# Attention and a gated convolution on one core: tiles 5 to 7 take the product with v on quarters of the array, with a new order of all work

## The chip, the cores and the metric

The kernel runs on one core of one Trainium2 chip. The metric is the device time of one execution in microseconds (us). Three runs of the kernel before gave 554.05, 554.26 and 555.79 us; the median is 554.26 us.

## The reference

Inputs are q, k and v (8 batches, 8 heads, 576 positions, 64 numbers a head) and three weights. What is computed, in short:

```python
scores = scale * q @ k.T                      # per batch and head
scores = where((rel >= 0) & (rel < 128), scores + slope[h] * -abs(rel), -1e9)
attn = exp(scores - max) ; attn = attn / (sum(attn) + 1e-9)
x = (attn @ v)                                # heads side by side: 576 x 512 per batch
h = maximum(x @ w_in, 0)                      # 512 -> 1024
conv = sum over 3 taps of conv_w[k] * h shifted by k - 1
out = (h * sigmoid(conv)) @ w_out             # 1024 -> 512
```

A position sees itself and the 127 positions before it, so a tile of 128 positions needs the keys of its own tile and of the tile before.

## The kernel before, in words

The 8 x 576 positions are 36 tiles of 128. For each tile the kernel turns q and k so that the head dimension lies on partitions, takes the scores (`scores`, L398 and L413), adds the position's bias (`add_bias`, L473, VectorE), takes exps (L481, ScalarE), normalises, turns the weights so that keys lie on partitions, and takes the product with v (`av`). The result is x, written as a high and a low part into `ring` (`x_hi`, `x_lo`). The network then runs on blocks of 256 positions, each in four steps of 256 of the 1024 features: up-projection (`up`, L692 and L697, name UH; its last number is the half of the step's features), relu (HH), convolution (Z, CA, CB, L732), tanh (TH), gate (GT), its high and low part (GH, GL), down-projection (`down`, L794 for the first steps, L804 later, name D), and after four steps the store of the output (OB, L830). The down-projection is TensorE's largest work.

Tiles before `FIRST` = 8 turn their weights on TensorE (`attnT`, L507) into the tiles `rl`; from tile 8 on the weights are turned by VectorE and through DRAM (TE, WE, SE, CE, tiles `eb`, `scr`, `rr`, `ll`). q and k are turned on TensorE before tile 8 (QU, L351, copied out by QV) and from tile 8 on by VectorE's transposes (`turn`, name TQ, L365) from the tiles `rp_late`, which small loads fill four at a time (LG, L315). The loads of q and k for the tiles before 8 are LD and LH, those of v LV (L341), of the weights F (L197).

The product with v exists in two forms. The old one (L631, tiles before 8) takes for each head and each of the two key tiles one product of 128 keys by 64 columns of v, all into one PSUM bank. `av_quarters` (L591, tiles from 8) cuts the array into four quarters of 64 by 64: the two key halves and two heads run beside each other, each key half into a PSUM bank of its own, and parts that the mask makes zero are left out. The two banks are then summed: ScalarE copies the first to the tile `xx` (XA, `x_part`, L186) and VectorE adds the second (XS, `x_sum`, L605). In the old form `x_hi` copies from PSUM and `x_lo` subtracts on VectorE (L659); in the quarter form `x_hi` copies from `xx` and `x_lo` subtracts on GpSimd (L657).

The order is written by hand: three lists of pieces, which `emit` walks, so that each engine and each DMA queue runs its instructions in the order of the list. OPENING has the first tiles, the preparation of weights and eleven steps' up-projections; PERIOD is emitted 14 times for two tiles and four steps each; TAIL ends the work. A name in the set `OTHER` puts that piece on its other engine (`pick`). `MB3.0.0` is piece MB on tile 3, with two indices of its own; in PERIOD the first number is added to the period's own tile or step. I is a spin, four matmuls on the identity that keep TensorE at work. SP issues all DMAs in the list's order.

Of the kernel before, what the change touches and what calls it, by code (L numbers as in the profile page):

```python
# [22 lines left out]
def tile_alibi_window_attention_conv_glu(  # L23
# [357 lines left out]
    def scores(t, u):  # L381
        if t >= TURN:
            if u == 0:
                for half in range(2):
                    scores_window(t, half)
            return
# [491 lines left out]
    LH0.0 LH0.1 LD1 F0 QU0.0 QU0.1 QV0.0 S0.0 MP0.0.0 F4 MP0.0.1 MB0.0.0 QV0.1 S0.1 LD2 MP0.1.1 LD3 MB0.0.1 MP0.1.0  # L878
    MB0.1.1 QU1.0 QU1.1 I2 QV1.0 I2 I2 LW0 MB0.1.0 S1.0 MP1.0.1 CL4 MP1.0.0 QV1.1 S1.1 MP1.1.0 MB1.1.0 MB1.0.1 QU2.1
    X0.0.0 X0.0.1 X0.1.1 X0.1.0 NR0 QV2.1 X1.1.0 N0.0 I1 I1 N0.1 X1.0.1 LW4 QU2.0 QV2.0 S2.1 MB1.0.0 CL0 S2.0  # L880
    MP1.1.1 X1.0.0 MB1.1.1 T0.1 RS4 X1.1.1 F1 CL1 LW1 MP2.1.1 MP2.0.0 MP2.0.1 NR1 T0.0 RL0.0 RL0.1 N1.1 N1.0 F2
    SEL0.0 V4 QU3.1 MB2.1.1 I1 I1 LV2 MB2.0.0 QV3.1 MP2.1.0 MB2.1.0 MB2.0.1 RS0 QU3.0 QV3.0 T1.1 P4 S3.1 SEL0.1
    MP3.1.0 MP3.1.1 RL1.1 MB3.1.0 SEL1.1 V0 S3.0 T1.0 RL1.0 LD4 QU4.0 X2.0.1 MB3.1.1 W4 I2 X2.1.1 CL2 MP3.0.1 X2.1.0
    QU4.1 LV0 X2.0.0 NR2 N2.1 N2.0 F3 AV0 XH0 QV4.1 QV4.0 MB3.0.1 H0 T2.0 RL2.0 LW3 X3.1.1 S4.0 MP3.0.0 MB3.0.0 T2.1
    LD5 S4.1 SEL1.0 CL3 SEL2.0 MP4.0.1 MB4.0.1 RL2.1 RS1 V1 RS3 RS2 LW2 MP4.0.0 SEL2.1 QU5.1 LV1 AV1 QV5.1 AV2 F6
    CL6 S5.1 XH1 QU5.0 MP4.1.0 MB4.1.0 X3.0.0 V3 X3.0.1 F8 MP4.1.1 MB4.1.1 MB4.0.0 CL8 X3.1.0 V2 F5 CL5 XH2 XL2 H1
    QV5.0 RS8 W1 LG4 UH1.0 NR3 N3.0 N3.1 MP5.1.1 UH1.1 X4.0.1 MP5.1.0 T3.1 HH1.0 X4.1.0 MB5.1.1 UH0.0 F7 CL7 LW5 W0
    MB5.1.0 F15 HH0.0 LW8 X4.1.1 X4.0.0 NR4 RL3.1 RS6 LD6 QU6.1 LW6 V6 LW7 RS7 V7 T3.0 QV6.1 V8 N4.0 LG4 LV4 RS5 V5
    HH1.1 RL3.0 SEL3.0 UH0.1 S5.0 MP5.0.0 HH0.1 LV3 F10 CL10 Z0.1 QU6.0 MP5.0.1 H7 F9 Z0.0 T4.0 RL4.0 H3 CA0.1 CB0.1
    LG4 UH3.0 HH3.0 N4.1 UH2.0 SEL4.0 CA0.0 T4.1 CB0.0 MB5.0.1 LD7 CL9 SEL3.1 X5.1.1 QV6.0 S6.0 MB5.0.0 HH2.0 TH0  # L890
    RL4.1 RS10 SEL4.1 X5.1.0 GT0 MP6.0.0 S6.1 MB6.0.0 Z1.0 MP6.0.1 AV3 H2 W3 X5.0.0 LW10 LG4 MP6.1.1 Z1.1 MB6.0.1
    LW9 AV4 H8 QU7.1 CA1.0 CB1.0 F12 LG4 X5.0.1 MP6.1.0 MB6.1.0 CA1.1 W2 CB1.1 NR5 N5.1 LV5 UH3.1 XH4 XL4 RS9 V9
# [5 lines left out]
    CA4.0 CB4.0 T6.0 TQ8 LG4 X7.0.1 RL5.0 LG4 UH6.0 TH4 GT4 LG4 LG4 GL2 LG4 SEL5.0 RL6.0 SEL6.0 V16 H16 T6.1 RL6.1
    SEL6.1 LW14 LG4 LG4 Z5.1 CA5.1 LG4 LG4 CB5.1 RS14 HH6 Z5.0 CA5.0 D1 CB5.0 RS15 RS13 AV5 XH5 HH7 GH4 BW0 V13 XL5
    V14 N7.0 AV6 XH6 TH5 GT5 Z6.0 S8.0 D2 LV9 H9 Z6.1 MP8.1.1 MB8.1.1 MP8.1.0 H12 V15 H15 LG4 LG4 CA6.1 MB8.1.0 T7.0  # L900
    RL7.0 D3 CB6.1 XL6 UH8.1 UH8.0 LG4 TQ9 X8.1.0 CA6.0 CB6.0 H14 UH9.1 W16 MP8.0.0 MB8.0.0 H11 W11 TH6 GT6 W9 H13
    GL4 Z7.1 CA7.1 CB7.1 MP8.0.1 Z7.0 HH8 MB8.0.1 W14 CA7.0 GH5 CB7.0 W13 X8.1.1 GL5 N8.1 TE8.1 S9.0 MP9.1.0 MP9.0.1
# [59 lines left out]
```

## Time and profile before

| what | value |
|---|---|
| median of three runs | 554.26 us |
| the profiled execution | 554.5 us |
| its span on the core | 552.8 us |
| TensorE busy | 546.0 us, 99% |
| VectorE, ScalarE, GpSimd busy | 446.8, 384.4, 342.5 us |
| mean granted TensorE clock | 0.999 |

The profiled execution's own time is 1.7 us above its span: what lies around the span. TensorE's matmuls are pipelined, so a busy TensorE need not be one at its peak. Engines other than TensorE matter where TensorE waits for them.

### The profile page before, as it was taken

The page shows a single profiled execution, that of the slowest core. Times are in us where ns is not written, and L with a number is a line of the kernel's source. Part 1 is how long each engine was busy: PE and PEld are TensorE (multiplying, and loading weights), DVE is VectorE, ACT ScalarE, POOL GpSimd, SP SyncE. Part 2 cuts the span into 40 slices and gives each one's busy share as a digit, 9 for nine tenths or more (in the row PEclk, how much of TensorE's full clock was granted, in tenths as well). Part 3 has the DMA queues.
Part 4 walks back from the last instruction along what each step waited for, and adds up shares of the span by engine and source line. Part 5 has one row for each costly group of instructions (what it writes and reads, how often), then busy time and mean ns, then how long its engine had stood idle before and what let it go on. Part 6 is the DMA issues. An engine that isn't in the chain of part 4 may idle for free.

```text
span 552.8 us, 17956 instructions
## 1 busy us (share of the span) xinstructions
PE 546.0 (99%) x6689; PEld 479.2 (87%) x6689; DVE 446.8 (81%) x1505; ACT 384.4 (70%) x1149; POOL 342.5 (62%) x450
## 2 busy tenths in 40 slices
PE   9999999999999999999999999999999999999997
PEld 8788886988888888888888888898989898989986
DVE  8899999888789977887596987788879987665763
ACT  5899876775867676868586776767676777664441
POOL 1787977594656575666558493948473948483241
PEclk9999999999999999999999999999999999999999
DMA  9987764546776767767676768676768664540102
GB/s 209 229 242 204 202 104 81 164 156 169 157 205 142 231 156 205 184 205 169 183 201 175 196 178 207 163 219 184 190 176 205 179 162 148 159 155 1 39 0 78
DMA packets 206779, 91.39 MB, mean 165 GB/s; under 512 B 178380, under 2 KB 192996, under 8 KB 206692
## 3 DMA queue, kind: packets, MB, share of 16 engines
q1 hardware_dynamic: 206692, 90.24, 62.5%
q8 instruction: 53, 0.87, 0.7%
q14 instruction: 34, 0.28, 0.2%
HBM read 51.40 MB, written 38.80 MB: 163 GB/s over the span
## 4 chain that ended last, share of the span: by engine, by line
PE 91%; DMA 2%; DVE 2%; SPq 2%; issue 1%; ACT 0%; DVEq 0%
PE o L804 34%; PE p L697 33%; PE av L591 7%; PE sc L413 6%; PE p L692 3%; PE o L794 3%; PE av L631 3%; PE sc L398 2%; SPq L341 1%; DMA wst<-in_moe_w_in_dram 1%; PE pa L507 1%; PE pt L351 1%; DVE zp L732 1%; DMA rp_late<-in_q_dram 1%; SPq L315 0%
## 5 line engine op out<-in xcount | busy, mean ns | idle before, releaser
L697 PE MATMUL p<-ring,wi 128*128 128x256 f32 x1088 | 195.8, 282 | 0.7 <-ACT hh L709 0.7
L732 DVE SCALAR_TENSOR_TENSOR zp<-hh,cw,zp 128x256 f32<-128x256 f32 (+7 forms) x384 | 160.4, 418 | 29.2 <-ACT zp L717 19.6
L697 PEld LDWEIGHTS p<-ring,wi 128*128 128x128 f32 x1088 | 168.4, 188 | 4.9 <-ACT hh L709 1.1
L697 PE MATMUL p<-ring,wl 128*128 128x256 f32 x544 | 152.3, 280 | 0.0
L768 POOL TENSOR_TENSOR gl<-z,gh 128x512 fp32r<-128x512 f32 x63 | 81.5, 1294 | 100.9 <-ACT gh L186 68.4
L481 ACT ACTIVATE e<-e,st 128x128 f32<-128x128 f32 x288 | 111.8, 391 | 4.2 <-DVE st L473 3.1
L804 PE MATMUL o<-wo,gh 128*128 128x512 f32 x270 | 110.0, 407 | 0.0
L501 POOL TENSOR_TENSOR e<-e,st 128x512 f32<-128x512 f32 x69 | 72.2, 1056 | 58.9 <-DVE st L493 54.1
L804 PE MATMUL o<-wo,gl 128*128 128x512 f32 x270 | 105.7, 392 | 0.0
L804 PE MATMUL o<-wl,gh 128*128 128x512 f32 x270 | 105.2, 390 | 0.0
L697 PEld LDWEIGHTS p<-ring,wl 128*128 128x128 f32 x544 | 102.7, 189 | 0.0
L739 ACT ACTIVATE zp<-zp 128x512 f32<-128x512 f32 (+1 forms) x73 | 42.2, 578 | 62.9 <-DVE zp L732 61.5
L717 ACT ACTIVATE zp<-hh,cw 128x256 f32<-128x256 f32 x144 | 68.5, 476 | 20.0 <-DVE z L747 10.0
L473 DVE CUSTOM_DVE_ANT_0 e<-sc,bias 128x128 f32<-128x128 f32 x288 | 66.8, 284 | 1.7 <-PE pa L507 0.2
L747 DVE SCALAR_TENSOR_TENSOR z<-zp,hh 128x512 f32<-128x512 f32 (+1 forms) x73 | 49.0, 671 | 21.1 <-ACT zp L739 20.2
L804 PEld LDWEIGHTS o<-wo,gh 128*128 128x128 f32 x270 | 50.6, 188 | 16.6 <-issue 6.7
L804 PEld LDWEIGHTS o<-wo,gl 128*128 128x128 f32 x270 | 50.5, 187 | 11.5
L804 PEld LDWEIGHTS o<-wl,gh 128*128 128x128 f32 x270 | 50.8, 188 | 9.3
L709 ACT ACTIVATE hh<-p 128x512 f32<-128x512 f32 (+2 forms) x69 | 39.5, 572 | 25.2 <-PE p L697 20.3
L481 ACT ACTIVATION_READ_ACCUMULATOR e<-e,st 128x1 f32 x288 | 54.5, 189 | 0.0
L186 ACT CAST gh<-z 128x512 fp32r<-128x512 f32 x58 | 35.6, 614 | 15.3 <-DVE z L747 15.3
L572 POOL TENSOR_SCALAR_AFFINE_SELECT rr<-rr 128x512 f32<-128x512 f32 x56 | 40.2, 722 | 3.4
(131 smaller groups left out, 882.5 us busy)
## 6 DMA issues: line engine op xcount, KB each, us to landing
scr<-eb SPq DMA_DIRECT2D x28, 1024.0 KB, 5.1
rr<-scr SPq DMA_DIRECT2D x112, 128.0 KB, 3.7
out_dram<-ob SPq DMA_DIRECT2D x17, 512.0 KB, 3.4
rv<-in_v_dram SPq DMA_DIRECT2D x32, 256.0 KB, 3.4
rp_late<-in_k_dram SPq DMA_DIRECT2D x192, 36.0 KB, 2.9
rp_late<-in_q_dram SPq DMA_DIRECT2D x192, 36.0 KB, 2.2
wst<-in_moe_w_in_dram SPq DMA_DIRECT2D x8, 512.0 KB, 7.0
wst<-in_moe_w_out_dram SPq DMA_DIRECT2D x8, 512.0 KB, 4.8
```

Of the source, the lines that this page charges most:

```text
L473: nc.vector.tensor_tensor_reduce(out=e[:, j, :], in0=of[:, g, :], in1=bias[:, u * HU + j, :], scale=-0.125, scalar=FAR, op0=ALU.add, op1=A ...
L481: nc.scalar.activation(out=e[:, j, :], in_=e[:, j, :], func=AF.Exp, bias=st[:, 0, j : j + 1], scale=-1.0, accum_out=st[:, 1, j : j + 1],)
L501: eng.tensor_tensor(out=e, in0=e, in1=st[:, 2, :].unsqueeze(2).to_broadcast([P, HU, P]), op=ALU.mult)
L572: nc.gpsimd.affine_select(out=r, in_=r, pattern=[[BK, 2], [0, H], [1, BK]], compare_op=ALU.is_ge, fill=0.0, base=q0, channel_multiplier=-1,)
L697: nc.tensor.matmul(ps, a[:, part], ring[:, i, cc, cols], start=cc == 0 and n == 0, stop=cc == NCC - 1 and n == 2)
L709: nc.scalar.activation(out=to, in_=ps, func=AF.Relu, scale=0.5)
L717: nc.scalar.activation(out=zps[s][:, ff, :], in_=hhs[s][:, ff, 1 : 1 + CW], func=AF.Copy, scale=cw[:, 1, f : f + 1])
L732: nc.vector.scalar_tensor_tensor(out=z[:, ff, a:cut], in0=hh[:, ff, a + kk : cut + kk], scalar=cw[:, kk, f : f + 1], in1=z[:, ff, a:cut], ...
L739: nc.scalar.activation(out=zps[s][:, ff], in_=zps[s][:, ff], func=AF.Tanh)
L747: nc.vector.scalar_tensor_tensor(out=zgs[s][:, ff], in0=zps[s][:, ff], scalar=1.0, in1=hhs[s][:, ff, 1 : 1 + CW], op0=ALU.add, op1=ALU.mult,)
L768: eng.tensor_tensor(out=gl, in0=zgs.pop(s), in1=as32(gh), op=ALU.subtract)
L804: nc.tensor.matmul(to, a[:, ff, ms], w[:, part], start=first and n == 0, stop=end and n == 2)
```

## The change

The product with v of tiles 5, 6 and 7 takes the quarter form. Their weights are still turned on TensorE, so the quarters read from `rl` through a new function `part_of`. The limits of `av`, `x_part`, `x_sum`, `x_hi` and `x_lo` go from `FIRST` (8) to `QUARTERS` (5). `TURN` and `SOLO` are 8, as `FIRST` is, and only give names to conditions that stay as they were. OPENING gets the pieces XA5, XS5, XA6 and XS6 (tile 7's are in the first period already), and all three lists and `OTHER` are ordered anew.

```diff
-    TURN = FIRST
+    TURN = 8
+    SOLO = 8
+    QUARTERS = 5
...
+    def part_of(t, side, h, rows, c, n):
+        if t >= FIRST:
+            return sides_of[t][side][rows, c // BK : (c + n) // BK, h, :]
+        return rls[t, h // HU][rows, side, h % HU, c : c + n]
...
                             vraw[t - side][rows, h + a],
-                            sides_of[t][side][rows, c // BK : (c + n) // BK, h + a, :],
+                            part_of(t, side, h + a, rows, c, n),
...
     def x_sum(t):
-        if t < FIRST:
+        if t < QUARTERS:
             return
...
     def x_part(t):
-        if t >= FIRST:
+        if t >= QUARTERS:
...
     def av(t):
-        if t >= FIRST:
+        if t >= QUARTERS:
             av_quarters(t)
             return
...
     def x_hi(t):
         ps, hi, lo = avs[t]
-        if t >= FIRST:
+        if t >= QUARTERS:
             copy_on(pick(nc.scalar, nc.gpsimd), hi, xs[t])
             return
...
         ps, hi, lo = avs.pop(t)
-        if t >= FIRST:
+        if t >= QUARTERS:
             pick(nc.gpsimd, nc.vector).tensor_tensor(out=lo, in0=xs.pop(t), in1=as32(hi), op=ALU.subtract)
             return
...
     OTHER = set(
...
-        QV2.0 QV3.0 RL1.0 RL3.1 RL5.1 RL6.1 T:GH-1 T:GH0 T:GH1 T:GH2 T:GH3 T:GH4 T:GH5.0 T:GH5.1 T:GL-1 T:GL0
...
+        GH7 GH8 GL5 H10 H11 H13 H3 H5 H6 H9 HH1.0 KC9 LW0 LW1 LW11 LW12 LW14 LW4 LW6 LW7 N4.1 N5.0 N8.0 N8.1
+        N9.0 P:GH0 QV3.0 QV4.0 QV7.0 RL0.1 RL6.0 T:GH-1 T:GH0 T:GH1 T:GH5.1 T:GL-1 T:GL1 T:GL3 T:GL5.0 T:GL5.1
+        T:HH0 T:HH5.0 T:OB1 T:OB5 T:XA-1 T:XH-1 W0 W13 XH0 XH2 XH5
...
     OPENING = """
...
+    SEL6.1 V16 HH6 LG4 Z5.1 LG4 SEL6.0 LG4 AV6 RS14 CA5.1 LG4 H16 LG4 LG4 H11 LG4 RS13 S8.0 V13 XA5 BW0 XS5 V15 XH5
+    XL5 LG4 XA6 XS6 XH6 X7.0.1 V14 D2 CB5.1 TH5 GT5 XL6 MP8.0.0 N7.0 Z6.0 H9 MP8.0.1 LG4 LG4 UH8.0 H14 MP8.1.1 CA6.0
...
     PERIOD = """
-    OB0 HH0 Z0.0 MB2.0.1 MB2.0.0 X2.0.0 UH1.1 UH1.0 HH1 X2.0.1 CA0.0 AV-1 TQ3 CB0.0 XA-1 XS-1 AV0 LG4 GH-1 GL-1 N2.0
...
+    HH0 UH1.0 MB2.0.0 Z0.0 UH1.1 MB2.0.1 HH1 GH-1 GL-1 X2.0.0 CA0.0 CB0.0 TQ3 Z0.1 LG4 AV-1 XA-1 XS-1 X2.0.1 CA0.1
...
     TAIL = """
...
+    UH1.0 HH0 Z0.0 CA0.0 AV-1 D-2 XA-1 XS-1 XH-1 Z0.1 CA0.1 XL-1 CB0.1 UH1.1 XF-1 UH3.0 CB0.0 TH0 UH2.1 HH1 GH-1 GT0
```

The order moves instructions at three places that matter below. The first is SP's queue in the opening, from its fifth DMA on (`rp_` tiles hold q and k, `wst_` a weight's words, `rv_` v). Before:

```order
L341 DMA rp_169<-in_q_dram 128x8x64
L341 DMA rp_169<-in_k_dram 128x8x64
L197 DMA wst_176<-in_moe_w_in_dram 128x1024
L197 DMA wst_199<-in_moe_conv_w_dram 24x256
L341 DMA rp_211<-in_q_dram 128x8x64
L341 DMA rp_211<-in_k_dram 128x8x64
L341 DMA rp_211<-in_q_dram 128x8x64
L341 DMA rp_211<-in_k_dram 128x8x64
L197 DMA wst_343<-in_moe_w_in_dram 128x1024
L197 DMA wst_366<-in_moe_w_in_dram 128x1024
L341 DMA rv_380<-in_v_dram 128x8x64
```

After the change:

```order
L197 DMA wst_187<-in_moe_conv_w_dram 24x256
L343 DMA rp_169<-in_q_dram 128x8x64
L343 DMA rp_169<-in_k_dram 128x8x64
L343 DMA rp_227<-in_q_dram 128x8x64
L343 DMA rp_227<-in_k_dram 128x8x64
L197 DMA wst_241<-in_moe_w_in_dram 128x1024
L197 DMA wst_273<-in_moe_w_in_dram 128x1024
L343 DMA rp_227<-in_q_dram 128x8x64
L343 DMA rp_227<-in_k_dram 128x8x64
L343 DMA rp_301<-in_q_dram 64x8x64 x2
L343 DMA rp_301<-in_k_dram 64x8x64 x2
L197 DMA wst_306<-in_moe_w_in_dram 128x1024
L343 DMA rv_358<-in_v_dram 128x8x64
```

The first full block of w_in (`wst_176`) leaves its place ahead of tile 1's q and k, and the next two blocks now stand ahead of tile 3's loads instead of behind them.

The second place is VectorE in the opening around the products of tiles 5 and 6 (`av_1367` and `av_1399` before, `av_1_1306` and `av_1_1371` now; L659 and L611 are lines of x's low part and of the sum; L225 prepares weights). Before:

```order
L188 COPY rl_1_1328<-pa_1_1323 128x512
L221 TENSOR_SCALAR wst_1010<-wst_1010 128x512
L732 SCALAR_TENSOR_TENSOR zp_1341<-hh_164,cw,zp_1341 128x256 x4
L225 SCALAR_TENSOR_TENSOR wg_1365<-wg_1365,wst_1002 128x512
L659 TENSOR_TENSOR ring<-av_1367,ring 128x4x128
L225 SCALAR_TENSOR_TENSOR wg_1353<-wg_1353,wst_1010 128x512
L493 RECIPROCAL st_0_1122<-st_0_1122 128x4
L188 CAST ring<-av_1399 128x4x128
L747 SCALAR_TENSOR_TENSOR z_1418<-zp_1341,hh_164 128x512
```

After the change:

```order
L221 TENSOR_SCALAR wst_1101<-wst_1101 128x512
L738 SCALAR_TENSOR_TENSOR zp_1286<-hh_164,cw,zp_1286 128x256
L225 SCALAR_TENSOR_TENSOR wg_1349<-wg_1349,wst_1147 128x512
L738 SCALAR_TENSOR_TENSOR zp_1286<-hh_164,cw,zp_1286 128x256
L225 SCALAR_TENSOR_TENSOR wg_1426<-wg_1426,wst_1038 128x512
L611 TENSOR_TENSOR xx<-xx,av_1_1306 128x512
L225 SCALAR_TENSOR_TENSOR wg_1299<-wg_1299,wst_722 128x512
L611 TENSOR_TENSOR xx<-xx,av_1_1371 128x512
L225 SCALAR_TENSOR_TENSOR wg_1404<-wg_1404,wst_1101 128x512
L738 SCALAR_TENSOR_TENSOR zp_1286<-hh_164,cw,zp_1286 128x256
L753 SCALAR_TENSOR_TENSOR z_1491<-zp_1286,hh_164 128x512
```

The two subtractions of L659 have left VectorE (the second stands a few rows below the piece shown), and two additions from PSUM (L611) stand in their place, among the same preparation of weights.

The third place is SP's queue in a period: loads of q (`rp_late`), of v, the store of an output block of 512 KB (`out_dram`), and the trip of the turned weights through DRAM (`scr`, `rr`). Before:

```order
L315 DMA rp_late<-in_q_dram 32x9x32 x4
L341 DMA rv_2294<-in_v_dram 128x8x64
L315 DMA rp_late<-in_q_dram 32x9x32 x12
L830 DMA out_dram<-ob_2352 128x2x512
L544 DMA scr_2375<-eb_2356 256x1x1024
L315 DMA rp_late<-in_k_dram 32x9x32 x8
```

After the change:

```order
L317 DMA rp_late<-in_q_dram 32x9x32 x4
L343 DMA rv_2411<-in_v_dram 128x8x64
L317 DMA rp_late<-in_q_dram 32x9x32 x8
L836 DMA out_dram<-ob_2424 128x2x512
L317 DMA rp_late<-in_q_dram 32x9x32 x4
L545 DMA scr_2442<-eb_2404 256x1x1024
L317 DMA rp_late<-in_k_dram 32x9x32 x8
```

Four of the period's q loads have moved from ahead of the output store to behind it. Everything else of the queue has kept its order.

## Rows read from the trace of the kernel before

**Rows 1.** The page, busy time by engine, clock by slices, chain by engine.

```profile
PE 546.0 (99%) x6689; PEld 479.2 (87%) x6689; DVE 446.8 (81%) x1505; ACT 384.4 (70%) x1149; POOL 342.5 (62%) x450
...
PEclk9999999999999999999999999999999999999999
...
PE 91%; DMA 2%; DVE 2%; SPq 2%; issue 1%; ACT 0%; DVEq 0%
```

**Rows 2.** The chain of waits, 80 to 250 us: start us, us, what.

```profile
83.68 3.64 PE av L631 x64
87.32 1.25 PE sc L413 x64
88.57 3.63 PE o L794 x8
...
121.72 1.90 PE av L631 x32
...
178.56 2.84 PE av L591 x128
```

**Rows 3.** Groups by line and shape: busy us, mean ns, idle before.

```profile
L657 POOL TENSOR_TENSOR ring<-xx,ring 128x512 fp32r<-128x512 f32 x27 | 34.3, 1291 | 1.4 <-ACT ring L186 1.4
...
L186 ACT CAST ring<-xx 128x512 fp32r<-128x512 f32 x28 | 17.5, 626 | 4.8 <-DVE xx L605 4.8
L605 DVE TENSOR_TENSOR xx<-xx,av 128x512 f32<-128x512 f32 x25 | 17.1, 686 | 12.9 <-ACT xx L186 12.8
L186 ACT COPY xx<-av 128x512 f32<-128x512 f32 x28 | 16.3, 583 | 1.7 <-PE av L591 0.9
...
L659 DVE TENSOR_TENSOR ring<-av,ring 128x512 fp32r<-128x512 f32 x6 | 4.1, 678 | 0.5 <-ACT ring L186 0.5
```

**Rows 4.** Busy us of each engine in 20-us stretches, clock, DMA share.

```profile
40.00:60.00 20.00, 20.00 (x186) 17.55 (x185) 18.29 (x63) 19.25 (x58) 15.43 (x20) 1.00 0.75 192
...
80.00:100.00 20.00, 20.00 (x194) 13.51 (x193) 18.70 (x50) 12.19 (x27) 13.12 (x21) 1.00 0.47 79
```

**Rows 5.** The timeline of PE in the opening: start, us, instructions, [idle before <-releaser].

```profile
19.60 0.63 PE L351 MATMUL pt<-ident_r,rp 128*128 128x128 f32 x4 [1.07 <-DVE st L473]
...
24.77 0.66 PE L351 MATMUL pt<-ident_r,rp 128*128 128x128 f32 x4 [0.26 <-DVE rl L188]
```

**Rows 6.** The timeline of DVE in the opening.

```profile
14.10 0.67 DVE L188 COPY qkT_all<-pt 128x512 f32<-128x512 f32 x1
...
17.36 0.43 DVE L221 TENSOR_SCALAR wst<-wst 128x512 uint32<-128x512 uint32 x1 [1.29 <-DMA wst<-in_moe_w_in_dram]
...
25.61 0.69 DVE L501 TENSOR_TENSOR e<-e,st 128x512 f32<-128x512 f32 x1
```

**Rows 7.** The chain of waits, where periods begin.

```profile
209.67 2.95 PE o L804 x12
...
237.94 2.95 PE o L804 x12
...
294.68 2.95 PE o L804 x12
...
324.21 2.95 PE o L804 x12
...
380.75 2.95 PE o L804 x12
...
408.56 2.95 PE o L804 x12
```

**Rows 8.** Waits of DVE on DMA: total us, times, longest.

```profile
DVE qkT_all L365 <- DMA rp_late<-in_q_dram: 4.6, 3, 3.6
DVE qkT_all L365 <- DMA rv<-in_v_dram: 3.1, 1, 3.1
```

**Rows 9.** DMA issues: KB of each, us from issue to landing.

```profile
out_dram<-ob SPq DMA_DIRECT2D x17, 512.0 KB, 3.4
```

**Rows 10.** The chain of waits in the tail.

```profile
516.16 2.75 PE o L804 x12
518.91 8.53 PE p L697 x72
```

More of the change, by code (lines that the diff above doesn't have):

```diff
@@ L381, in scores @@
     def scores(t, u):
[L382 to L385, printed above, removed]
+        if t >= FIRST:
+            for half in range(2) if t >= SOLO else (u,):
+                scores_window(t, half)
             return
@@ L434, in place @@
         ps = sms[t, u][2][a]
-        if t >= TURN:
+        if t >= FIRST:
             place_window(t, ps)
@@ L877, in tile_alibi_window_attention_conv_glu @@
     OPENING = """
[L878 to L892, printed above, removed]
@@ L898, in tile_alibi_window_attention_conv_glu @@
[L898 to L902, printed above, removed]
@@ new lines, in tile_alibi_window_attention_conv_glu @@
+    X0.0.0 LD2 I2 MB0.1.1 MB0.0.1 X0.1.1 I2 I1 F0 S1.0 CL4 MP0.1.0 S1.1 MB0.1.0 MP1.0.0 MP1.0.1 X0.0.1 F1 QU2.1
+    QU2.0 LD3 MB1.0.1 MB1.0.0 X0.1.0 NR0 N0.0 QV2.1 CL0 LW4 MP1.1.0 LD4 F2 MP1.1.1 MB1.1.1 N0.1 S2.1 MP2.1.1 MB1.1.0
+    QV2.0 S2.0 X1.0.1 X1.0.0 I1 X1.1.1 X1.1.0 MP2.0.0 CL1 T0.0 MP2.1.0 MB2.1.0 LV0 LW1 LW0 QU3.1 NR1 T0.1 N1.1 RS4
+    V4 RL0.0 QV3.1 MB2.1.1 X2.1.1 RL0.1 SEL0.0 MB2.0.0 I1 QU3.0 I1 T1.1 SEL0.1 F3 QV3.0 MP2.0.1 LD5 MB2.0.1 S3.1
+    MP3.1.0 S3.0 MP3.1.1 N1.0 X2.0.0 MB3.1.1 MB3.1.0 RL1.1 SEL1.1 RS0 CL2 X2.1.0 P4 V0 W4 X2.0.1 LV1 NR2 T1.0
@@ new lines, in tile_alibi_window_attention_conv_glu @@
+    MP3.0.1 MB3.0.1 QU4.0 RL1.0 QV4.0 MP3.0.0 MB3.0.0 X3.1.0 QU4.1 QV4.1 AV0 XH0 N2.0 T2.0 S4.0 MP4.0.0 RL2.0 LW3
+    MB4.0.0 X3.1.1 S4.1 F8 X3.0.1 MP4.1.1 I2 QU5.1 N2.1 MP4.1.0 X3.0.0 MB4.1.0 RS1 V1 SEL2.0 CL3 T2.1 RL2.1 SEL1.0
+    AV1 X4.0.0 LV2 SEL2.1 AV2 F7 MP4.0.1 RS2 CL8 LW2 NR3 MB4.1.1 XH1 H0 V2 QV5.1 S5.1 MB4.0.1 F6 LV3 RS3 XH2 RS8
+    N3.1 LG4 X4.0.1 F5 X4.1.1 LD6 N3.0 QU5.0 H1 QV5.0 V3 UH1.0 T3.1 XL2 UH1.1 CL6 X4.1.0 LW6 UH0.1 LW5 W0 W1 HH1.0
+    MP5.1.1 MP5.1.0 MB5.1.0 LW7 RL3.1 QU6.1 F15 CL5 RS5 V5 HH1.1 UH0.0 NR4 N4.1 HH0.1 CL7 RS7 N4.0 LG4 QU6.0 LW8 RS6
@@ new lines, in tile_alibi_window_attention_conv_glu @@
+    SEL6.1 V16 HH6 LG4 Z5.1 LG4 SEL6.0 LG4 AV6 RS14 CA5.1 LG4 H16 LG4 LG4 H11 LG4 RS13 S8.0 V13 XA5 BW0 XS5 V15 XH5
+    XL5 LG4 XA6 XS6 XH6 X7.0.1 V14 D2 CB5.1 TH5 GT5 XL6 MP8.0.0 N7.0 Z6.0 H9 MP8.0.1 LG4 LG4 UH8.0 H14 MP8.1.1 CA6.0
+    LV9 MB8.1.1 Z6.1 GH4 X7.1.0 X8.1.1 MB8.0.1 MP8.1.0 MB8.1.0 X8.1.0 CA6.1 H13 CB6.1 CB6.0 TH6 GT6 H15 T7.0 RL7.0
+    LV7 UH8.1 LG4 GL4 Z7.1 TQ9 CA7.1 W11 MB8.0.0 GH5 Z7.0 CA7.0 N8.1 CB7.0 X8.0.0 HH8 D3 GL5 TE8.1 UH9.1 CB7.1 W16
+    S9.0 MP9.0.1 W9 OB3 MP9.1.1 MP9.1.0 X7.1.1 N7.1 MP9.0.0 MB9.1.0 MB9.0.1 D4 T7.1 X8.0.1 N8.0 SEL7.0 TH7 GT7 W13
@@ L926, in tile_alibi_window_attention_conv_glu @@
+    GL0 UH4.1 GT2 UH3.1 GH2 GL2 HH3 Z3.0 CA3.0 CB3.0 Z3.1 CA3.1 CB3.1 TH3 D-1 D0 HH4 Z4.0 Z4.1 GH1 GL1 GT3 GH3 CA4.0
+    CA4.1 CB4.1 GL3 D1 OB1 HH5.1 CB4.0 TH4 GT4 UH5.0 GH4 HH5.0 GL4 Z5.1 D2 Z5.0 CA5.0 CB5.0 TH5.0 CA5.1 GT5.0 CB5.1
+    GH5.0 GL5.0 D3 TH5.1 D4 GT5.1 GH5.1 GL5.1 D5 OB5
     """
@@ L930, in tile_alibi_window_attention_conv_glu @@
         emit(OPENING)
-        for t in range(FIRST, NT, 2):
-            emit(PERIOD, t, 2 * (t - FIRST) + 10, "P:")
-        emit(TAIL, NT, 2 * (NT - FIRST) + 10, "T:")
+        for t in range(SOLO, NT, 2):
+            emit(PERIOD, t, 2 * (t - SOLO) + 10, "P:")
+        emit(TAIL, NT, 2 * (NT - SOLO) + 10, "T:")
 _INS = ["q", "k", "v", "moe_w_in", "moe_conv_w", "moe_w_out"]
```

48 lines of the change are left out of this document (24 added, 24 removed).

## The prediction

> **What bounds the kernel now.** I read the page first, for its shares and its chain [rows 1]: TensorE is busy 99% of the span at a clock that never leaves full speed (2.4 GHz), and 91% of the chain that ends last is TensorE's. So only two things change the time: TensorE gets less to do, or it waits less or more. Next I read the chain of waits, for what the product with v costs in each of its forms [rows 2], and the groups by shape, for what the new pieces cost on the other engines [rows 3]. The table by stretches [rows 4] tells how much room those engines have at that place. Then I looked for TensorE's waits. They lie in the opening, where the two timelines show them [rows 5, 6], and in the middle, where the distance between periods gives them [rows 7]: a normal period takes 237.94 - 209.67 = 28.27 us and the one with tile 27, which opens a batch, 408.56 - 380.75 = 27.81. The two periods from 237.94 to 294.68, one of them with tile 18, took 56.74 where 28.27 + 27.81 = 56.08 are normal, and the next one 29.53. So the middle loses 0.66 + 1.26 = 1.92 us, and the list of VectorE's waits has the cause: its transposes of q and k waited 3.6 and 3.1 us for loads [rows 8]. Elsewhere every period is TensorE's own work, without a wait.
>
> **The product with v of tiles 5 to 7.** In the old form tiles 5 and 6 take 3.64 us together and tile 7 takes 1.90 [rows 2]. In the quarter form two tiles take 2.84 in a period [rows 2], 1.42 each, with 64 records instead of 32 for each tile. So the three go from 3.64 + 1.90 = 5.54 to 3 x 1.42 = 4.26: **-1.3 us**, all on the path, since TensorE does not pause there (20.00 us busy of 20 from 80 to 100) [rows 4]. The tiles have the same shape and masks as those of a period; only the tile that the weights come from differs. At worst that different source gives nothing (0), at best it is the whole 1.3.
>
> The Trainium skill, "TensorEngine Tiling (Array Packing)", section Instruction Overhead, gives every matmul on trn2 about 60 cycles; at 2.4 GHz an estimate by that page is 64 x 25 ns = 1.6 us for a tile, and the three would gain 5.54 - 4.8 = 0.7 us. The trace disagrees with it: 2.84 us for 128 records is 22 ns for each, so the measured 1.42 stands.
>
> **What the quarter form adds elsewhere.** For each tile ScalarE copies a bank (0.58 us), VectorE adds the other (0.69), the high part is copied from the sum (0.63 on ScalarE) and the low part is taken by GpSimd in 1.29 instead of by VectorE in 0.68 [rows 3]. From 80 to 100 us ScalarE is busy 12.19 of 20 and GpSimd 13.12 [rows 4], so both have room; VectorE at 18.70 gives up a subtraction for an addition of the same length. I cost these at nothing. What hides them is TensorE's work up to the first user. After the products come the scores of tile 8, which want four PSUM banks, and a down-projection, 1.25 + 3.63 = 4.88 us [rows 2]; then the up-projection UH8.0 reads tile 6's low part. The chain for tile 6 is 0.58 + 0.69 + 0.63 + 1.29 = 3.19 us [rows 3], to which XA5 and XS5 ahead of it on the same two engines add up to 0.7 of queueing: some 3.9 of 4.88. If weight preparation on VectorE (it stands between XS5 and XS6) holds it a further microsecond, that cover is gone and TensorE waits. I take 0, with an end of +0.7 (one more subtraction's length, 0.68) [rows 3].
>
> **The opening.** Before its last wait ends at 24.77 us, TensorE waits for VectorE 1.07 and 0.26 us, together 1.33 [rows 5]. In the same stretch VectorE has 1.29 us of waiting for a block of w_in and two pieces of 0.67 and 0.69 (QV2.0, a copy of turned q and k; N2.0, a normalisation) [rows 6]. The new order issues that block two loads earlier and takes both pieces off VectorE; a copy of the same kind (QV4.0, priced by that row at 0.67) comes to it. VectorE could so be ahead by up to 1.29 + 0.67 + 0.69 - 0.67 = 1.98, at the very best 2.65 without the last. The other end is 0: q, k and v of the next tiles may simply arrive last instead. It can even cost a little, because ScalarE gets the pieces and is busy 19.25 of 20 us from 40 to 60 [rows 4]. I take **-1.3**, the TensorE waits that the timeline names, since after them TensorE never pauses and more lead on VectorE has nothing to shorten.
>
> **Periods.** TensorE's order in a period is unchanged but for the halves of one up-projection, and no added wait stands in it. So 28.27 stays. What moves is SP's queue: four q loads that stood ahead of the 512 KB store now stand behind it, and the store takes 3.4 us from issue to landing [rows 9]. The transposes that use these loads stand in the next period. They now come behind one instruction more on VectorE, and the two places where such loads were late (1.92 us) may get better or worse. For the middle I take **0**, with ends of -1.92 (both gone) and, as a rival, +6.8.
>
> **Tail.** The down-projection D-2 (2.75 us) [rows 10] and one half of an up-projection still stand between the last tile's product and its first user, so 0.
>
> **Sum.** -1.3 - 1.3 = -2.6 us. The profiled execution's own time is 554.5 (span 552.8 and 1.7 around it), 0.2 above the median of the runs, 554.26. Against it 551.9 in a profiled execution, and **551.7 us** as a median. This kernel's measurement tells some 0.3% from no change, 1.7 us.
>
> **The rivals.**
>
> *Only the product gets shorter.* The opening's lead is eaten by loads or by ScalarE. For: 19.25 of 20 us of ScalarE [rows 4], and DMAs that land as late as before. Against: TensorE's two waits name VectorE as the releaser [rows 5]. 554.26 - 1.3 = 553.0, within 0.3%.
>
> *The new order also clears the middle.* The two late loads are where a search over orders could still gain. -1.3 - 1.92 and an opening between -1.3 and -1.98 give 549.1 to 549.7, say 549.5. Against: each q group now has a store ahead of it.
>
> *Slower: the q loads come too late.* Behind the store the four loads land up to 3.4 us later [rows 9]; VectorE's transpose waits, and behind it in VectorE's queue stand the convolution and the masks that TensorE's next steps need. The two periods that lose 0.66 and 1.26 show the point from which it decides: waits of 3.6 and 3.1 us were absorbed up to 2.9 and 1.8 [rows 7, 8]. Past that all is paid. If only these two periods get 3.4 more each, TensorE loses 6.8: 554.26 - 2.6 + 6.8 = 558.5. Against: in the other periods the transposes hardly wait at all (a total of 4.6 and 3.1 us in the whole run) [rows 8], so there is slack of its own before the first microsecond counts.
>
> *The sum of two banks becomes the bound.* The Trainium skill, "TensorEngine Tiling (Array Packing)", section PSUM Bottleneck, holds that tiling quickens TensorE but not the emptying of PSUM, which can become the bottleneck. Here it would be UH8.0 waiting behind the chain above and the scores of tile 8 waiting for banks. By the rows it costs up to 0.7 once, and it lies inside the cases above: with the opening's gain it gives 554.26 - 2.6 + 0.7 = 552.4, still faster; with the first rival 553.7, within 0.3%.
>
> **How the numbers follow.** The forecast with its variants has 0.42, the cleared middle 0.18, the product alone 0.25, the late loads 0.15. Faster by over 0.3% is below 552.6: the first two, 0.60. Within: 0.25. Slower: 0.15. The range runs from 549.2, the cleared middle in its better half, to 555.2: the product's gain, nothing from the opening, one more stall of 1.26 in the middle [rows 7] and the wait of UH8.0 (554.26 - 1.3 + 1.26 + 0.7 = 554.9), and a little for an opening that loses.
>
> **What would show it.** The profile after should have groups of 128 records with 2.84 us or 64 with some 1.5 where the old form stood near 85 us, and the old form only on tiles 0 to 4. TensorE's last wait of the opening should end some 1.3 us earlier. Period starts should stand 28.27 apart (27.81 with tiles 18 and 27), and the two stretches of 56.74 and 29.53 tell about the middle. I am wrong if TensorE waits after the products of tiles 5 and 6 by over a microsecond, if several periods exceed 28.27 with VectorE's transposes waiting on q loads, or if the opening's waits only change their name.

## The result and the profile after

The changed kernel takes 560.69 us (median of 4 runs, 560.18 to 561.43); the kernel before took 554.15 in the runs beside it. The ratio is 1.0112, 95% interval 1.0092 to 1.0133: 6.5 us slower where 2.6 faster was forecast, outside the range. Two things that the prediction had priced low took the time: loads of q that come late, as in the rival that had 0.15 (that the store makes them late is not shown), and the added copies and sums, the rival that was thought small.

The page of the changed kernel, its busy times and its chain by engine:

```profile
PE 546.0 (98%) x6785; PEld 478.7 (86%) x6785; DVE 445.8 (80%) x1502; ACT 379.1 (68%) x1141; POOL 356.7 (64%) x467
...
PE 62%; DVE 13%; SPq 9%; DMA 5%; POOL 4%; issue 3%; ACT 2%; DVEq 0%; ACTq 0%; POOLq 0%
```

TensorE is busy just as long as before, 546.0 us [rows 1], in a span of 559.3 instead of 552.8. So the 6.5 us are waiting. A little more than that is, since the products are shorter and the busy time is not: some short waits are counted as busy. The chain tells the same: TensorE has 62% of it instead of 91% [rows 1], and VectorE, SP's queue and the DMAs have the rest.

Where the time went is best seen from the down-projection, whose 854 matmuls come in the same order in every kernel here; at those chosen, the work of TensorE ahead of them is the same too. The lag is the start of one of them less the start of the same one in the profiled execution of the kernel before. In the first line stand that matmul's number and, in brackets, its start before in us; the second is the changed kernel's lag in us:

```
matmul          1 (66.7)  97 (130.3)  121 (144.5)  217 (200.6)  433 (329.4)  841 (547.5)
after            -0.14       1.55        1.35         3.96         4.08         4.94
```

Five stretches: the opening up to 67 us gave nothing; the products of tiles 5 to 7 and what stands around them cost 1.5 to 1.7 instead of giving 1.3; one period lost 2.6; the next 130 us came out as before; and one more period lost 0.8 (the lag is 4.09 before it and 4.86 behind). The last 1.6 us of the difference lie behind TensorE's last matmul: it ends at 554.5, 4.8 us before the span's end, where 549.6 and 3.2 us stood before. In eleven of the twelve runs below the span's difference is the lag at the end (with the orders alone 555.6 - 552.8 = 2.8 and a lag of 2.81), and in one (copies_first) 1.4 us are added as here. Why, and whether every execution of the changed kernel has it, is open.

First the products. TensorE's timeline in the changed kernel:

```profile
83.48 1.57 PE L597 MATMUL av<-rl,rv 64*64 64x128 f32 x64
85.26 1.57 PE L597 MATMUL av<-rl,rv 64*64 64x128 f32 x64 [0.21 <-POOL rl L522]
86.76 1.53 PE L414 MATMUL sc<-qkT_all 64*32 64x160 f32 x64
88.22 3.70 PE L800 MATMUL o<-wg,z 128*128 128x512 f32 x8
...
92.39 0.39 PE L703 MATMUL p<-ring,wi 128*128 128x256 f32 x1 [0.36 <-POOL ring L663]
...
123.77 1.45 PE L597 MATMUL av<-rl,rv 64*64 64x128 f32 x56 [0.95 <-ACT hh L715]
```

The products of tiles 5 and 6 last 1.57 us each, near the 1.5 that the prediction named as the sign of the quarter form: from 83.48 to 86.76 they take 3.28 with a wait of 0.21, where the old form took 3.64 [rows 2]. But waits follow: 0.36 ahead of the up-projection UH8.0 for GpSimd's low part (L663), 0.95 within the product of tile 7 for ScalarE's relu (L715), which empties a PSUM bank, and some smaller ones. The busy time of the engines in the stretch, in the changed kernel and then in the run with the new orders and the old form (`orders_alone`, below):

```profile
80.00:100.00 20.00, 19.43 (x253) 12.56 (x253) 15.93 (x45) 16.90 (x48) 19.14 (x26) 1.00 0.41 67
```

```profile
80.00:100.00 20.00, 19.84 (x188) 13.06 (x187) 16.71 (x47) 15.76 (x46) 15.90 (x22) 1.00 0.44 71
```

GpSimd is now busy 19.14 of 20 us and ScalarE 16.90, where 13.12 and 12.19 stood [rows 4]. The new orders alone bring them to 15.90 and 15.76, and the form adds the rest. VectorE goes down from 18.70 to 15.93, most of it with the orders alone (16.71). So the room that the prediction read from the old order was not there in the new one.

Then the period. The chain of waits of the changed kernel between 183 and 200 us:

```profile
183.29 3.17 DMA rp_late<-in_q_dram
...
186.92 0.65 DVE xx L611
...
188.38 1.04 POOL e L502
189.42 2.52 POOL ring L663 x2
...
192.25 7.35 PE p L703 x60
```

It starts with a q load that lands late, at 186.46, and goes on through VectorE's sum of two banks, GpSimd's normalisation and its two low parts to the up-projection. The transposes that wait, in the kernel before and after:

```profile
180.47 0.45 DVE L365 STREAM_TRANSPOSE qkT_all<-rp_late 128x256 f32<-128x256 f32 x1 [0.33 <-DMA rp_late<-in_q_dram]
```

```profile
186.55 0.45 DVE L367 STREAM_TRANSPOSE qkT_all<-rp_late 128x256 f32<-128x256 f32 x1 [3.32 <-DMA rp_late<-in_q_dram]
```

The wait there was 0.33 us and is 3.32. In the whole run the transposes now wait much more than in [rows 8]:

```profile
DVE qkT_all L367 <- DMA rp_late<-in_q_dram: 14.5, 5, 4.2
```

The period starts of the changed kernel, against [rows 7]:

```profile
213.63 2.95 PE o L810 x12
...
242.29 2.95 PE o L810 x12
...
299.22 2.95 PE o L810 x12
...
328.29 2.95 PE o L810 x12
...
384.84 2.95 PE o L810 x12
...
412.64 2.95 PE o L810 x12
...
469.96 2.95 PE o L810 x12
```

213.63 to 242.29 is 28.66, the next two together 56.93 (56.08 normal), then 29.07, then two of 28.27 and one of 27.80. Over normal that is 0.39, 0.85 and 0.80, together 2.04 where 1.92 stood before: the middle is as it was. The two periods from 412.64 to 469.96 take 57.32, 0.78 over normal.

### The profile page after: what moved, and what is told of

Read it like the earlier page. It is cut to its first block, busy times and chain, and to the rows that moved or that the text cites. A ratio compares the mean times of both kernels' runs of the same rounds, so it can differ in the third digit from the quotient of the medians.

```text
span 559.3 us, 18132 instructions
## 1 busy us (share of the span) xinstructions
PE 546.0 (98%) x6785; PEld 478.7 (86%) x6785; DVE 445.8 (80%) x1502; ACT 379.1 (68%) x1141; POOL 356.7 (64%) x467
## 4 chain that ended last, share of the span: by engine, by line
PE 62%; DVE 13%; SPq 9%; DMA 5%; POOL 4%; issue 3%; ACT 2%; DVEq 0%; ACTq 0%; POOLq 0%
PE o L810 23%; PE p L703 22%; SPq L317 8%; PE av L597 5%; PE sc L414 4%; DVE zp L738 4%; PE p L698 3%; DMA rp_late<-in_q_dram 2%; DVE e L474 2%; DVE qkT_all L367 2%; POOL e L502 1%; POOL ring L663 1%; PE av L637 1%; DVE sc L464 1%; SPq L559 1%
## 5 line engine op out<-in xcount | busy, mean ns | idle before, releaser
L502 POOL TENSOR_TENSOR e<-e,st 128x512 f32<-128x512 f32 x67 | 70.5, 1054 | 51.3 <-DVE st L494 43.0
L474 DVE CUSTOM_DVE_ANT_0 e<-sc,bias 128x128 f32<-128x128 f32 x288 | 68.7, 284 | 1.5 <-POOL wst L204 0.2
L715 ACT ACTIVATE hh<-p 128x512 f32<-128x512 f32 (+1 forms) x74 | 41.8, 568 | 29.4 <-PE p L703 25.7
L367 DVE STREAM_TRANSPOSE qkT_all<-rp_late 128x1024 f32<-128x1024 f32 (+3 forms) x37 | 36.0, 977 | 17.6 <-DMA rp_late<-in_q_dram 14.5
```

The source lines that it names most:

```text
L367: nc.vector.transpose(out=slots_of(t)[:, :, :, m * BK : end * BK].rearrange("p i g (m c) -> p i g m c", c=BK), in_=groups[n][:, :, :, at : ...
L474: nc.vector.tensor_tensor_reduce(out=e[:, j, :], in0=of[:, g, :], in1=bias[:, u * HU + j, :], scale=-0.125, scalar=FAR, op0=ALU.add, op1=A ...
L502: eng.tensor_tensor(out=e, in0=e, in1=st[:, 2, :].unsqueeze(2).to_broadcast([P, HU, P]), op=ALU.mult)
```

## The experiments

Two theories stood at the start. "Late loads": the new orders make SP issue loads of q and k later, VectorE's transposes wait, and TensorE behind them. "Two banks": the copies and sums of the quarter form hold TensorE up. The lags of all runs, in us, at the same matmuls as above:

```
matmul                        1      97     121     217     433     841
orders_alone              -0.33    0.82    0.64    2.46    2.12    2.81
quarters_alone             0.79    2.06    2.06    2.41    2.39    2.39
old_periods               -0.36    1.29    2.33    2.33    2.74    2.74
new_period_alone          -0.07   -0.06   -0.26    1.09    1.13    1.54
loads_ahead               -0.33    1.03    0.84    2.30    3.93    5.69
new_period_loads_ahead    -0.70   -0.71   -0.90   -0.91   -0.59   -0.20
copies_first              -0.08    1.69    2.15    2.15    2.05    2.05
tile7_alone                0.50   -0.02    0.15    0.96   -0.50    0.77
loads_ahead_and_opening    0.08    1.47    1.28    3.09    3.95    4.03
tile7_v_behind_q           0.33   -0.20   -0.02    4.06    8.86   14.18
weights_first              0.99    2.11    2.58    2.58    4.19    4.20
tile7_again               -0.25   -0.78   -0.60   -0.60   -2.49   -1.73
```

Eight of these have the old opening up to the products, and their first column runs from -0.70 to 0.99: that much one profiled execution differs from another there. The runs tile7_alone and tile7_again are two executions of the same kernel. They agree in what they gain up to matmul 97 (0.52 and 0.53) and differ by 2.5 us at the end (0.77 and -1.73). So from matmul 121 on a lag tells where one execution lost time; whether the kernel always loses it there, one trace does not tell.

### The orders and the quarter form apart

```diff
-    QUARTERS = 5
+    QUARTERS = 8
```

> The changed kernel with the limit for the quarter form back at tile 8: its new orders alone, with the old form of the product on tiles 5 to 7. Theory 'late loads' (the new orders make SP issue the loads of q and k later, so VectorE's transposes wait for them): the loss comes from the orders, so 559 to 562 us, and TensorE again falls behind by some 2.6 us between 180 and 205 us. Theory 'two banks' (the copies and sums of the quarter form on tiles 5 to 7 hold TensorE up): the loss goes away, 554 to 555.5 us.

Measured: 558.35 us, ratio 1.0076 (1.0049 to 1.0102). Between the two theories: the orders by themselves cost some 4 us; in the trace 1.8 of them lie between the matmuls 121 and 217. The form on top of them costs 2.3 more (560.69), with intervals that overlap a little.

The quarter form in the old orders has this edit (and `QUARTERS = 5`):

```diff
-    AV5 XH5 HH7 GH4 BW0 V13 XL5 V14 N7.0 AV6 XH6
+    AV5 XA5 XS5 XH5 HH7 GH4 BW0 V13 XL5 V14 N7.0 AV6 XA6 XS6 XH6
```

> The kernel before with its own orders, and only the quarter form on tiles 5 to 7 (XA5 XS5 behind AV5, XA6 XS6 behind AV6 in the opening). 'Late loads': 552.5 to 554 us, the gain of the product in full or in part and no new wait in the periods. 'Two banks': 557 us or more, with TensorE waiting behind the products of tiles 5 to 7.

Measured: 557.34 us, ratio 1.0056 (1.0038 to 1.0074). The quarter form costs 3 us by itself, so each theory holds a part. TensorE's timeline of that run:

```profile
84.39 2.91 PE L597 MATMUL av<-rl,rv 64*64 64x128 f32 x128
87.23 1.25 PE L414 MATMUL sc<-qkT_all 64*32 64x160 f32 x32
88.86 0.46 PE L414 MATMUL sc<-qkT_all 64*32 64x160 f32 x2 [0.38 <-ACT hh L715]
89.95 0.77 PE L414 MATMUL sc<-qkT_all 64*32 64x160 f32 x30 [0.63 <-ACT xx L186]
90.65 3.70 PE L800 MATMUL o<-wg,z 128*128 128x512 f32 x8
```

The two products take 2.84 us (84.39 to 87.23), exactly as forecast, 0.8 less than before. But the scores of tile 8, which took 1.25 us [rows 2], now take 3.42 (87.23 to 90.65). They need four PSUM banks of five, the two products hold four, and ScalarE empties them in its own order:

```profile
88.22 0.59 ACT L715 ACTIVATE hh<-p 128x512 f32<-128x512 f32 x1
88.70 0.61 ACT L186 CAST gh<-z 128x512 fp32r<-128x512 f32 x1
...
89.32 0.57 ACT L186 COPY xx<-av 128x512 f32<-128x512 f32 x1
```

The copy of tile 6's first bank (XA6) starts at 89.32, although the product ended at 87.3: a relu, a high part of the gate and the high part XH5, which waits for VectorE's sum, stand ahead of it. The second half of the scores starts when that copy is done, at 89.95.

### The new period and the new opening apart

> The changed kernel with the period and the tail of the kernel before, so only its opening (with the quarter form) is new. If the new opening is what makes the loads late: 556 to 560 us, with a loss between 110 and 210 us. If the new period does (q loads behind the store): 552.5 to 555 us.

Measured: 557.55 us, ratio 1.0060 (1.0039 to 1.0081): the new opening with the quarter form, and the old period and tail. Its lag is there at matmul 121 (2.33), does not grow near 185 us (2.33 at 217) and grows by 0.4 later. The time lies within the first expectation, but in this trace the place is another: of the loss between 110 and 210 us 1.04 came between the matmuls 97 and 121, and none near 185, where the transpose waited only 0.99.

> The kernel before with only the new period (old opening and tail, old form on tiles 5 to 7). If the new period makes the loads late: 556 to 560 us, several periods longer than 28.27 us with the transposes waiting for q. If the opening does: 553.5 to 555.5 us.

Measured: 555.85 us, ratio 1.0036 (1.0023 to 1.0050), just under the range of the first theory: the new period costs something by itself. In the trace the lag grows by 1.35 us between 121 and 217, at the same place as in the changed kernel, and the transpose waits there as it does in it:

```profile
183.64 0.45 DVE L367 STREAM_TRANSPOSE qkT_all<-rp_late 128x256 f32<-128x256 f32 x1 [3.08 <-DMA rp_late<-in_q_dram]
```

### The store and the q loads

In the new period the third four of the twelve q loads stand behind the store OB1. The edit moves SP's queue alone:

```diff
-    MB4.1.1 OB1 CB3.0 CB3.1 TE3.1 LG4 LG4
+    MB4.1.1 CB3.0 CB3.1 TE3.1 LG4 OB1 LG4
```

> The run with the new period alone, with the same move of OB1 behind the next LG4. It lost 1.35 us between 180 and 205 us and some 0.4 near 440. By the store: back to 553.5 to 554.8 us. By another part of the period's order: 555.5 us or more, as without the move.

Measured: 555.55 us, ratio 1.0011 (0.9988 to 1.0034; 1.0036 without the move). The median lies at the other theory's edge, the interval reaches to no change, and it overlaps with that of the run without the move: the time does not decide it. In the one trace the lag does not grow between 121 and 217 (-0.90, -0.91), and the wait is gone:

```profile
180.33 0.45 DVE L367 STREAM_TRANSPOSE qkT_all<-rp_late 128x256 f32<-128x256 f32 x1 [0.42 <-DMA rp_late<-in_q_dram]
```

But one trace does not decide it either. The kernel with the quarter form on tile 7 alone (below) has the old period, with all twelve q loads ahead of the store. It was traced twice, and the same transpose waited 3.08 us in the first execution and 0.48 in the second:

```profile
183.37 0.45 DVE L367 STREAM_TRANSPOSE qkT_all<-rp_late 128x256 f32<-128x256 f32 x1 [3.08 <-DMA rp_late<-in_q_dram]
```

```profile
180.02 0.45 DVE L367 STREAM_TRANSPOSE qkT_all<-rp_late 128x256 f32<-128x256 f32 x1 [0.48 <-DMA rp_late<-in_q_dram]
```

The wait of this transpose in every trace, and what TensorE lost between the matmuls 121 and 217, both in us, the second against the kernel before. `tile7_v_behind_q` has no number in the second column, since it waited for v there (below):

```
twelve q loads ahead of the store         wait   lost
tile7_v_behind_q                          0.26      -
before                                    0.33   0.00
new_period_loads_ahead                    0.42   0.01
tile7_again                               0.48   0.00
old_periods                               0.99   0.00
weights_first                             1.34   0.00
copies_first                              1.50   0.00
quarters_alone                            2.60   0.35
tile7_alone                               3.08   0.81
loads_ahead                               3.25   1.46
loads_ahead_and_opening                   3.59   1.81
four of them behind the store
new_period_alone                          3.08   1.35
after                                     3.32   2.61
orders_alone                              3.56   1.82
```

All three traces with loads behind the store wait for over 3 us, but so do three of the eleven without. So the store is not needed for the wait, and that it is the cause in the new period is likely and not shown. The loss goes with the wait: waits up to 1.50 cost nothing, those from 2.60 on cost 0.35 to 2.61, in the old period too.

> The changed kernel with one move in the period: the piece OB1 goes behind the next LG4, so that on SP all twelve q loads stand ahead of the output's store again. No other engine's order changes. If the four q loads behind the store are what the period near 185 us loses (2.6 us) and the one near 440 (0.8 us): 556.5 to 558.5 us, the transpose's wait near 183 us under 1.5 us. If the position of the transpose on VectorE does it: 559.5 us or more.

Measured: 559.23 us, ratio 1.0081 (1.0052 to 1.0109), 1.5 us under the changed kernel. It lies between the two expectations, and the wait did not go:

```profile
184.90 0.45 DVE L367 STREAM_TRANSPOSE qkT_all<-rp_late 128x256 f32<-128x256 f32 x1 [3.25 <-DMA rp_late<-in_q_dram]
```

The q load now lands 1.6 us earlier, but VectorE asks 1.6 us earlier for it too, so it waits 3.25 instead of 3.32. In this kernel the loads were late without the store.

> The run with the loads ahead of the store, and two moves on SP in the opening besides: the fetch F14 goes ahead of the four k loads before it (two 512 KB fetches no longer stand side by side), and the v load LV7 goes behind the last four q loads. If the late start of the loads in the new opening is what still makes the transposes wait (the first transpose at 96.3 us against 92.2 before, and 1.5 us lost near 185): the first transpose by 95 us, the loss near 185 us under 0.8 us, 557 to 558.7 us. If not: 559 us or more and the loss near 185 stays over 1.2 us.

```diff
-    GL1 LG4 F14 LW12
+    GL1 LG4 LW12
...
-    QV7.1 KC7 S7.1
+    QV7.1 KC7 F14 S7.1
...
-    LV7 UH8.1 LG4 GL4
+    UH8.1 LG4 LV7 GL4
```

Measured: 558.82 us, ratio 1.0106 (1.0075 to 1.0136). A miss: the transpose that the expectation calls the first (TQ9; TQ8 stands ahead of it) came at 96.72, and the loss near 185 was 1.81. The loads did start earlier (the last k load ahead of that transpose was issued at 92.1 instead of 93.9), and the transpose, which waits for no load there, came no earlier. So the start of the loads in the opening is not what holds it. What the traces show besides is a loop. The next group's loads write into tiles that a transpose must first have read. In the kernel before, that transpose on VectorE, and SP's next k loads:

```profile
122.52 1.38 DVE L365 STREAM_TRANSPOSE qkT_all<-rp_late 128x256 f32<-128x256 f32 x2
```

```profile
122.99 1.44 SPq L315 DMA_DIRECT2D rp_late<-in_k_dram  x3
```

and in the changed kernel:

```profile
126.36 1.37 DVE L367 STREAM_TRANSPOSE qkT_all<-rp_late 128x256 f32<-128x256 f32 x2
```

```profile
126.83 1.32 SPq L317 DMA_DIRECT2D rp_late<-in_k_dram  x3
```

The load follows 0.46 or 0.47 us behind the start of the first of the two transposes, 0.03 behind its end, in all fourteen traces (also 123.24 and 123.70 with the new period alone, 126.00 and 126.47 with the orders alone). With the new opening VectorE comes to that transpose 2.7 to 3.8 us later than before, while TensorE is only 0.8 to 1.6 late (matmul 97); so the loads start late. That VectorE's lag is what makes the q loads land late near 185 was not tried by taking it away, and with the old opening `tile7_alone` has that late landing with a transpose only 0.5 us late (123.03). What makes the loads near 185 late in one execution and not in another stays open.

### The banks

> The run with the quarter form alone, in another order of pieces that were already there: the relu HH7 ahead of AV5, and both bank copies XA5 and XA6 ahead of the high parts and weights (HH7 AV5 XA5 AV6 XA6 XS5 GH4 BW0 V13 XH5 XS6 XL5). If tile 8's scores waited for PSUM banks that ScalarE empties late, the stretch from the product of tile 5 to the down-projection behind the scores shrinks from 6.3 us to 4.5 to 5.2, and the time to 553 to 555.5 us. If the wait has another origin, both stay: 6 us or more, 556.5 us or more.

```diff
-    AV5 XA5 XS5 XH5 HH7 GH4 BW0 V13 XL5 V14 N7.0 AV6 XA6 XS6 XH6
+    HH7 AV5 XA5 AV6 XA6 XS5 GH4 BW0 V13 XH5 XS6 XL5 V14 N7.0 XH6
```

Measured: 558.01 us, ratio 1.0060 (1.0040 to 1.0079). TensorE's timeline:

```profile
83.54 2.91 PE L597 MATMUL av<-rl,rv 64*64 64x128 f32 x128
86.38 1.72 PE L414 MATMUL sc<-qkT_all 64*32 64x160 f32 x64
88.02 4.04 PE L800 MATMUL o<-wg,z 128*128 128x512 f32 x8
91.90 0.60 PE L508 MATMUL pa<-ident_r,e 128*128 128x128 f32 x4
...
100.36 1.97 PE L414 MATMUL sc<-qkT_all 64*32 64x160 f32 x64
```

The expected stretch came out: 83.54 to 88.02 is 4.48 us, where 6.26 stood. The time did not follow. From the start of the next down-projection to the next piece are 3.88 us (88.02 to 91.90), 3.54 in the run below, for weights that VectorE prepares behind the sums. The wait is that of a weight load (PEld):

```profile
90.08 0.30 PEld L800 LDWEIGHTS o<-wg,z 128*128 128x128 f32 x2 [0.90 <-DVE wg L225]
```

And the scores of tile 9 stretch over 1.97, where a tile's scores take 1.25 [rows 2]. The wait had moved to the next work. So the late bank is shown as the cause of the stretch, but not of the whole loss.

> The run with the copies first, and on VectorE the two pieces of weight preparation V13 and V14 ahead of the two sums XS5 and XS6 instead of between and behind them. Theory 'VectorE's queue': a sum that waits for ScalarE's copy holds up all that stands behind it on VectorE, which has no room in this stretch; with work that is ready ahead of it, the lag of TensorE behind the kernel before at 111 us (1.68 us there) falls to 0.9 or less, and the time to 555.5 to 557 us. Theory 'too much work': the added sums and copies are simply too much for VectorE and ScalarE there, whatever the order: lag of 1.4 us or more, 557.5 us or more.

```diff
-    XS5 GH4 BW0 V13 XH5 XS6 XL5 V14 N7.0
+    V13 V14 XS5 GH4 BW0 XH5 XS6 XL5 N7.0
```

Measured: 556.62 us, ratio 1.0043 (1.0028 to 1.0057), within "VectorE's queue". Its timeline:

```profile
84.62 2.91 PE L597 MATMUL av<-rl,rv 64*64 64x128 f32 x128
87.45 1.01 PE L414 MATMUL sc<-qkT_all 64*32 64x160 f32 x32
88.82 0.78 PE L414 MATMUL sc<-qkT_all 64*32 64x160 f32 x32 [0.35 <-DVE xx L611]
89.53 3.70 PE L800 MATMUL o<-wg,z 128*128 128x512 f32 x8
93.07 0.60 PE L508 MATMUL pa<-ident_r,e 128*128 128x128 f32 x4
```

The scores wait 0.35 us and the down-projection is back at 3.54 (89.53 to 93.07). The lag grows by 1.12 from matmul 1 to 97, where it grew by 1.77 with the copies first and 1.27 with the quarter form alone. That is over the 0.9 that was set (which did not reckon with a lag of 0.99 at the start) and under the 1.4 of the other theory. The interval overlaps with that of the copies first (1.0040 to 1.0079). So VectorE's order is likely part of the cost, and what is left is not shown to be order or load.

### Tile 7 alone

> The kernel before with the quarter form on tile 7 alone (old orders). The pair of tiles 7 and 8 goes from 3.40 to 2.84 us. If nothing behind it is late: 553.3 to 554 us. If the down-projection behind it waits for a part of w_out that GpSimd prepares later (as in the run with all three, where 0.45 went), 553.8 to 554.5 us. Over 555 us would say that the form costs by itself.

With `QUARTERS = 7` and the old orders: 554.22 us, ratio 0.9989 (0.9969 to 1.0008). The chain of waits:

```profile
122.24 2.84 PE av L597 x128
125.08 2.97 PE o L810 x12
```

Before, tile 7 took 1.90 [rows 2] and tile 8 behind it 1.50:

```profile
123.62 1.50 PE av L591 x64
```

So the pair takes 2.84 us instead of 3.40, and the lag falls by 0.52 to matmul 97.

> The same kernel as the run with the quarter form on tile 7 alone, with more rounds, since it is the one candidate that beats both kernels. Its products gained 0.53 us where they stand. If nothing else moves: 553.2 to 553.9 us against a kernel before of 554.05. If its small waits elsewhere take it back: 554 us or more.

Measured: 554.17 us, ratio 0.9987 (0.9973 to 1.0001). Twice the same sign, and an interval that just reaches 1: a gain of 0.5 us that is likely and not shown.

> The run with the quarter form on tile 7 alone, and in the period the v load LV2 behind the twelve q loads instead of in their midst. If a load behind the q loads only has to land later and the q loads' landing is what the middle loses (0.66 and 1.26 us): the waits near 270 and 305 us shrink, 552.3 to 553.6 us, better than both kernels. If the v load then comes late itself or the q loads wait for buffers: 554 us or more.

```diff
-    N3.0 LG4 LV2 MP4.0.1
+    N3.0 LG4 MP4.0.1
...
-    OB-2 LG4 CA3.1
+    OB-2 LG4 LV2 CA3.1
```

Measured: 568.24 us, ratio 1.0266 (1.0232 to 1.0301). The second case, far over its bound: the transposes wait less for q (2.0 us in all, 7.3 without the move), and TensorE waits for v instead:

```profile
PE av L597 <- DMA rv<-in_v_dram: 5.2, 3, 2.0
```

At 182.31 the product starts after a wait of 2.22 us; the v load was issued at 178.89, behind the sixteen q loads, and landed at 182.08. In a period SP issues one DMA behind the other (in the kernel before from 209.38 to 239.15 with hardly a gap), so what is put ahead is paid by what is put behind.

## Why the prediction was wrong, point by point

- **The product.** Right in its size: 2.84 us for two tiles in the run of the quarter form alone, as the rows of tiles 8 and later said, and 0.52 for tile 7. The 22 ns for a record, read from the rows, held, and not the estimate of 25.
- **"I cost these at nothing."** This step failed. The cover was compared with the length of one chain, 3.2 to 3.9 us against 4.88, and the first user was taken to be UH8.0. The first user is the scores of tile 8, which stand straight behind the products and need the banks these hold: they cost 2.2 us in the old orders, more than the product gains. The chain's length was taken without what stands ahead of each piece in its engine's queue. The bank rival was priced at 0.7. In the old orders the form's added pieces, of which the bank is one, made TensorE 1.1 to 1.8 later from matmul 1 to 97 (three runs), where the product alone would have made it 1.3 earlier, and 3 us slower in the measured time. In the new orders that stretch loses 1.15 without the form (orders_alone) and 1.69 with it, so the form adds 0.5 where it should have given 1.3. In the changed kernel the scores of tile 8 lose only 0.2 (86.76 to 88.22 instead of 1.25), and the form's cost lies in the waits for GpSimd's low part and ScalarE's relu shown above. Why the order alone costs 1.15 stays open. The Trainium skill, "TensorEngine Tiling (Array Packing)", section PSUM Bottleneck, warns that the copy out of PSUM can become the bottleneck after tiling. The run of the quarter form alone agrees: there the scores waited for ScalarE's copy of a bank until 89.95.
- **The opening, -1.3.** It did not come. The lag at the first down-projection is -0.14 in the changed kernel and -0.36 to 0.08 in the other four with that opening, against -0.70 to 0.99 with the old one: on average some 0.4 us earlier, within the spread. TensorE's waits only changed their names [rows 5]. The timeline of the changed kernel's opening:

```profile
19.94 0.66 PE L508 MATMUL pa<-ident_r,e 128*128 128x128 f32 x4 [0.62 <-POOL e L502]
...
23.34 0.63 PE L508 MATMUL pa<-ident_r,e 128*128 128x128 f32 x4 [0.60 <-DVE st L474]
...
31.22 2.04 PE L637 MATMUL av<-rl,rv 128*64 128x128 f32 x33 [1.07 <-POOL rl L522]
```

  They are 2.29 us for a normalisation on GpSimd, a bias addition on VectorE and a mask on GpSimd, where 1.33 stood. And VectorE left the opening later than before (its transpose TQ9 at 96.51 instead of 92.20); whether the periods paid for that was not tried.
- **The periods, 0.** Right for the middle (2.04 us over normal, 1.92 before), wrong by 2.6 us in the period near 185 and 0.8 near 445. This step failed too: the four q loads were held to have slack of their own there. The rival named late q loads, and they came, but at another place than the two periods that had lost time before. That the store makes them late is not shown: an execution with the old period waited as long as the one with the new period alone (3.08). The prediction's point of 1.8 to 2.9 us that are absorbed would price the wait of 3.32 at 0.4 to 1.5; TensorE lost 2.61 in the changed kernel and 0.81 to 1.82 in the five other traces with a wait of over 3 us.
- **The tail, 0.** Right: the lag is 4.86 ahead of it and 4.94 at its end.

The sum from the changed kernel's one trace, in lags: the opening -0.1, the stretch of the products 1.5 (order and form together), the period near 185 2.6, near 445 0.8, the rest to 4.94 0.2, and 1.6 behind the last matmul that no run explains. By the measured times the orders alone cost 4.3 of the 6.5 us, and most of how they do it is open.
